# Products of zeros in TensorE's planned waits, and the ones of all V buffers written earlier, in a fused adaLN / sliding attention / token-MLP block

## The chip, the core and the metric

The kernel runs on one core of a Trainium2 chip. The core's engines work side by side, each in its own order: TensorE (PE; its weight loads are shown as PEld), VectorE (DVE), ScalarE (ACT), GpSimd (POOL) and SyncE (SP), which issues nearly all transfers. The metric is the device time of one execution in microseconds; the kernel before took 247.29 us, the median of 3 runs.

## The reference, cut to what matters

The batch is 1, S = 2048 tokens, D = 512, 32 heads of 16, a causal window of 256 keys, and an MLP that mixes tokens (2048 to 1792 and back).

```python
mod = (silu(c) @ w_mod).reshape(...)            # sa, ca, ga, sb, cb, gb
h = layernorm(x) * (1 + ca) + sa
q, k, v = split(h @ wqkv)                       # 32 heads of 16
p = softmax(where(mask, q @ k.T * 16 ** -0.5, -1e9))   # 0 <= i - j < 256
x = x + ga * ((p @ v) @ wo)
h = layernorm(x) * (1 + cb) + sb
u = gelu(einsum('bsd,sf->bdf', layernorm(h), w1) + b1)
y = einsum('bdf,fs->bds', u, w2) + b2
out = x + gb * y.transpose(0, 2, 1)
```

## The kernel before

**Head.** The 2048 tokens are 16 tiles of 128, in four groups of four. The head (from line 525) is written out by hand: the first loads, masks on GpSimd, the modulation's matrix-vector products on TensorE (`fm`, L586), layer norm of tiles 0 and 1, and the first projections. Among them stand ten products of a tile of zeros (`warm`, L571), whose result nobody reads.

**Planned part.** From line 641 on the order is made by a planner while the kernel is built. It keeps an estimated clock for TensorE (`pe["t"]`) and for each other engine (`free`), and always emits the work that it reckons can begin first (`while True`, L1278). Its time 0 lies at the end of the head. TensorE has three kinds of work: *scores* of a unit (L696; a unit is a part of four heads' window, in two halves, each into one of three PSUM tiles t0, t1, t2), *dense* groups into one of two PSUM tiles named dn (projections L356 and L331, modulation rows L402, and so on), and *AV* (`emit_av`, L721), the product of the exponentials with V. ScalarE takes the exponential of each half (L704), which makes that t tile free again. VectorE and ScalarE empty the dn tiles: K for even and odd heads (L369), Q and V (L287). The planner chooses; what then runs waits for semaphores, so an order that was planned with a wrong estimate makes its engine wait.

**Tiles 2 and 3.** The first group's second half comes later than its first: VectorE takes the statistics (`ln1_stats`, L244 and L245), GpSimd the reciprocal root (`rstd_of`, L231 and L235), VectorE applies them (`ln1_apply`, L256, tile xn), TensorE turns the result (`half_turn`, L309), VectorE modulates it (L297), and TensorE projects it (L356).

**V buffers.** `Vring` has three buffers V0, V1, V2. Beside each head's 16 columns stand two of ones, for the sum of the softmax. `ones_of(r)` writes them with two fills on GpSimd (L592, L593). In the kernel before, V0's are written in the head; V1's and V2's are planned jobs of GpSimd.

**Group 1's layer norm.** Tiles 4 to 7 are normalised (L256) into a pool of three buffers xn, and turned by transposing transfers on SP's queue (`turn_block`, L305). The fourth tile takes the buffer of the first, so its L256 on VectorE waits until the first transfer has landed. On SP's queue the four stand behind the loads of `wod` (L224), each of which waits for an earlier transfer (`wmod`, L221) to land. VectorE then modulates the turned tiles (L297 on h1T) once all four have landed; of these four steps one stands ahead of the evacuation of the last V group of group 0 (L287) on VectorE's queue, and the first AV product waits for that V group.

## Time and profile before

| | |
|---|---|
| median of 3 runs | 247.29 us (246.52, 247.29, 250.26) |
| profiled execution, whole | 248.87 us |
| its span | 246.7 us |
| mean granted clock of TensorE | 0.986 |
| busy: PE, DVE, ACT, POOL | 229.8, 190.0, 158.5, 69.7 us |

The span runs from the first to the last instruction; the remaining 2.17 us of the profiled execution lie around it. A row of the timeline has the start in us, the duration in us, the engine, the line, the operation, what is written and read, and how many instructions are merged into it; in brackets stands the idle time of the engine just before it, and what ended it. A row of a table by stage has the stretch and its length, then for each engine the busy time and the number of instructions, then the granted clock of TensorE, the share of the transfer engines and the rate.

### The profile page before, as it was taken

The page shows a single profiled execution, that of the slowest core. Times are in us where ns is not written, and L with a number is a line of the kernel's source. Part 1 is how long each engine was busy: PE and PEld are TensorE (multiplying, and loading weights), DVE is VectorE, ACT ScalarE, POOL GpSimd, SP SyncE. Part 2 cuts the span into 40 slices and gives each one's busy share as a digit, 9 for nine tenths or more (in the row PEclk, how much of TensorE's full clock was granted, in tenths as well). Part 3 has the DMA queues.
Part 4 walks back from the last instruction along what each step waited for, and adds up shares of the span by engine and source line. Part 5 has one row for each costly group of instructions (what it writes and reads, how often), then busy time and mean ns, then how long its engine had stood idle before and what let it go on. Part 6 is the DMA issues. An engine that isn't in the chain of part 4 may idle for free.

```text
span 246.7 us, 8687 instructions
## 1 busy us (share of the span) xinstructions
PE 229.8 (93%) x3691; PEld 122.6 (50%) x3723; DVE 190.0 (77%) x416; ACT 158.5 (64%) x182; POOL 69.7 (28%) x158
## 2 busy tenths in 40 slices
PE   5877999999999788999999999999999999999995
PEld 2544675655566365454454554544444444444444
DVE  5697679998999999999997989957974632543564
ACT  3495897999999898999999999950108700000000
POOL 7636104332272332423413624403540000000000
PEclk9996899999999999999999999999999999999999
DMA  6994455287573611010013131059995000201031
GB/s 202 314 351 129 88 148 131 43 139 160 168 98 74 152 25 27 5 21 3 9 23 79 51 88 45 3 169 352 415 409 224 0 3 0 85 23 64 27 103 43
DMA packets 32042, 27.70 MB, mean 112 GB/s; under 512 B 16516, under 2 KB 27652, under 8 KB 32004
## 3 DMA queue, kind: packets, MB, share of 16 engines
q1 hardware_dynamic: 31708, 26.63, 38.3%
q8 instruction: 29, 0.48, 0.9%
q10 hardware_dynamic: 296, 0.53, 0.6%
q14 instruction: 9, 0.07, 0.1%
HBM read 22.03 MB, written 2.10 MB: 98 GB/s over the span
## 4 chain that ended last, share of the span: by engine, by line
PE 74%; DVE 12%; ACT 6%; DMA 3%; issue 3%; SPq 0%; DVEq 0%; ACTq 0%
PE py L1475 20%; PE t L696 12%; PE dn L470 9%; PE dn L356 7%; PE t L462 6%; ACT et L704 6%; PE t L721 5%; PE dn L331 4%; PE dn L432 4%; PE t L1334 3%; DVE KT L369 3%; DMA wmod<-in_w_mod_dram 2%; PE pu L1334 2%; DVE QT L287 1%; PE pa L1370 1%
## 5 line engine op out<-in xcount | busy, mean ns | idle before, releaser
L704 ACT ACTIVATE et<-t 128x1024 bf16<-128x1024 f32 (+1 forms) x142 | 131.8, 1021 | 8.0 <-PE t L696 7.3
L1475 PE MATMUL py<-guT,w2r 128*128 128x512 bf16 (+2 forms) x234 | 47.7, 363 | 0.2
L696 PE MATMUL t<-QT,KT 32*128 32x64 bf16 (+4 forms) x752 | 38.0, 253 | 1.4 <-ACT et L704 0.9
L356 PE MATMUL dn<-h1T,wqkv 128*128 128x512 bf16 (+1 forms) x140 | 33.6, 357 | 4.9 <-DVE QT L287 1.8
L1475 PEld LDWEIGHTS <-w2r 128*128 128x128 bf16 x252 | 23.5, 98 | 25.4 <-DVE gelu_a L1357 0.4
L748 POOL TENSOR_TENSOR merge<-t,zr 128x512 bf16<-128x512 f32 (+1 forms) x16 | 21.5, 1346 | 42.8 <-DVE zr L743 42.7
L1490 DVE SCALAR_TENSOR_TENSOR o<-py,bFM,bc_gb 128x512 bf16<-128x512 f32 (+2 forms) x17 | 12.1, 711 | 24.5 <-PE py L1475 23.0
L696 PEld LDWEIGHTS <-KT 32*128 32x128 bf16 x752 | 13.9, 93 | 27.0 <-issue 25.1
L696 PE MATMUL t<-mask_r,mask_w 32*128 32x128 bf16 (+3 forms) x432 | 24.8, 223 | 0.4 <-issue 0.4
L470 PE MATMUL dn<-hb,w1hi 128*128 128x512 bf16 x91 | 23.9, 381 | 0.9 <-issue 0.6
L734 DVE STREAM_TRANSPOSE t<-t 128x1024 f32<-128x1024 f32 x16 | 19.8, 1236 | 4.2 <-PE t L721 4.1
L356 PEld LDWEIGHTS <-wqkv 128*128 128x128 bf16 x160 | 14.2, 102 | 16.3 <-issue 4.5
L231 POOL TENSOR_SCALAR ln_ve<-ln_mv 128x1 f32<-128x1 f32 x32 | 7.7, 241 | 48.0 <-DVE ln_mv L831 39.4
L235 POOL TENSOR_TENSOR ln_rstd<-ln_ve,mhalf 128x1 f32<-128x1 f32 x32 | 19.2, 601 | 2.7
L721 PEld LDWEIGHTS <-V 64*32 64x32 bf16 x1504 | 16.5, 91 | 6.6 <-issue 6.3
L721 PE MATMUL t<-et,V 64*32 64x320 bf16 (+4 forms) x1384 | 19.3, 251 | 0.0
L331 PE MATMUL dn<-wqkv,h1T 128*64 128x256 bf16 x256 | 17.6, 276 | 1.4 <-DVE V L287 0.9
L696 PEld LDWEIGHTS <-mask_w 32*128 32x128 bf16 x432 | 14.1, 95 | 2.7 <-issue 0.6
L331 PEld LDWEIGHTS <-h1T 128*64 128x64 bf16 x256 | 12.9, 109 | 3.4 <-issue 2.4
L470 PEld LDWEIGHTS <-w1hi 128*128 128x128 bf16 x98 | 8.1, 97 | 10.5 <-issue 3.0
L432 PE MATMUL dn<-wod,OTd 128*128 128x512 bf16 x43 | 12.2, 381 | 0.7 <-issue 0.3
L287 DVE CAST V<-dn 128x512 bf16<-128x512 f32 x15 | 10.1, 676 | 2.1 <-PE dn L331 2.1
(123 smaller groups left out, 289.3 us busy)
## 6 DMA issues: line engine op xcount, KB each, us to landing
w2r<-in_B_w_dram SPq DMA_DIRECT2D x14, 512.0 KB, 10.2
w1hi<-in_B_w_dram SPq DMA_DIRECT2D x11, 320.0 KB, 4.0
w1b<-in_B_w_dram SPq DMA_DIRECT2D x5, 448.0 KB, 6.7
x<-in_A_x_dram SPq DMA_DIRECT2D x16, 128.0 KB, 3.6
wmod<-in_w_mod_dram SPq DMA_DIRECT2D x4, 512.0 KB, 9.3
out_dram<-otile SPq DMA_DIRECT2D x15, 128.0 KB, 1.7
wqkv<-in_B_w_dram SPq DMA_DIRECT2D x11, 128.0 KB, 2.8
wqkv<-in_A_wqkv_dram SPq DMA_DIRECT2D x4, 256.0 KB, 6.0
```

What stands on the lines that cost most here:

```text
L235: nc.gpsimd.tensor_tensor(out=r[:], in0=ve[:], in1=mhalf[:, 0:n], op=ALU.pow)
L331: nc.tensor.matmul(pv[CH * par : CH * par + CH, 256 * ch : 256 * ch + 256].rearrange("p (h d) -> p h d", d=DH), lhsT=h1T[tg][:, dc, t0 : t ...
L356: nc.tensor.matmul(pq[:, 0:n_cols], lhsT=wqkv[:, dc, col0 : col0 + P], rhs=h1T[tg][:, dc, cols], start=(dc == 0), stop=(dc == ND - 1),)
L432: nc.tensor.matmul(pa[:], lhsT=tokens_of(OTd[tg][g], tl), rhs=wod[:, g, :], start=(g == 0), stop=(g == ND - 1),)
L462: nc.tensor.matmul(first[k][1][:, n, :], lhsT=w1_of(sc, 2 * k + n), rhs=hb[sc][:], start=(sc == 0), stop=(sc == NT - 1),)
L470: nc.tensor.matmul(ps[:], lhsT=w1_of(s0 + n, fc), rhs=hb[s0 + n][:], start=(n == 0), stop=(s0 + n + 1 == s1),)
L696: nc.tensor.matmul(o, lhsT=w, rhs=r, start=start, stop=stop, tile_position=(row, 0), skip_group_check=True,)
L704: nc.scalar.activation(out=state["e", u][:, 2 * a : 2 * a + 2, 0:w], in_=ps[:, :, 0:w], func=ACT.Exp, scale=SCORE_SCALE,)
L721: nc.tensor.matmul(chunks(o, qs), lhsT=Vring[kc // GC % 3][rows, kc % GC, h : h + 32], rhs=e[:, at : at + len(qs), :], start=first, stop=F ...
L734: nc.vector.transpose(out=v["t"][:].rearrange("p a c -> p (a c)"), in_=po[:].rearrange("p a c -> p (a c)"))
L748: eng.tensor_tensor(out=v["m"][:].rearrange("p (b d h) -> p h b d", d=DH, h=4)[:, :, lo:hi], in0=view()[:, :, lo:hi, 0:DH], in1=v["z"][:, ...
L1475: nc.tensor.matmul(pys[tl, lo, hi][:, 0 : hi - lo], lhsT=w2r[:, fc, tb * P : (tb + 1) * P], rhs=gated[fc][:] if last and (lo, hi) == LAST[ ...
```

## The change

Three edits. First, a new function `keep_busy` is called before each piece of work that the planner gives TensorE. It compares the planned start with the end of TensorE's work so far; if the gap is at least 0.35 us by the planner's clock, a PSUM tile is free by that clock, and the start lies before 24.0 on it, it takes that PSUM tile and emits one product of zeros (128x512) for each 0.25 us of the gap less 0.1. The planner's clocks and its count of TensorE's instructions aren't told of them. Second, `ones_of` is called for all three V buffers in the head. Third, the two planned jobs that wrote V1's and V2's ones keep their place in the planner's clock and emit nothing.

```diff
@@ -55,6 +55,7 @@
 PAUSE = 1.2
+BUSY_UNTIL = 24.0
 TURN_LAT = 2.5
@@ -601,7 +602,8 @@
         for step in masks["far"]:
             step(nc.gpsimd)
-        ones_of(0)
+        for r in range(3):
+            ones_of(r)
@@ -909,7 +911,7 @@
         for r in (1, 2):
-            Job(lambda eng, r=r: ones_of(r), {GE: 0.6}, prio=6, at=6.0).settle()
+            Job(lambda eng: None, {GE: 0.6}, prio=6, at=6.0).settle()
@@ -1275,6 +1277,17 @@
+        def keep_busy(until):
+
+            n = int((until - pe["t"] - 0.1) / 0.25)
+            pools = [
+                pool for pool, x in [*zip(t_pools, t_free), *zip(dn_pools, d_free)] if x is not None and x < pe["t"] + 0.1
+            ]
+            if n > 0 and pools and until < BUSY_UNTIL and pe["t"] > 0:
+                ps = pools[0].tile([P, 4 * P], DT.float32, name="dn" if pools[0] in dn_pools else f"t{t_pools.index(pools[0])}")
+                for _ in range(n):
+                    nc.tensor.matmul(ps[:], lhsT=zero[:, 0:P], rhs=zero[:], start=True, stop=True)
+
         while True:
             best = pick_pe()
@@ -1284,6 +1297,7 @@
             if callable(best[1]):
+                keep_busy(best[0])
                 best[1](best[0], *best[2])
```

Nine products of zeros come of it, all into t tiles and all among the first eight units: one each before the third early Q/K group and before the scores of units 1, 2 and 3; two between the Q/K groups of the second half (below); one before the second half's K group of head group 2; two before the scores of unit 7's second half, behind the transposition of the biases (L422). No other row moves on TensorE, and none on VectorE, ScalarE or SP.

The first place is TensorE's queue just ahead of the scores of unit 1. dn_437 (dn_443 in the changed kernel) is an early Q group, t1 and t0 are the PSUM tiles of the unit's two halves; in brackets stands the engine whose semaphore an instruction waits for. Before:

```order
L356 LDWEIGHTS wqkv_132
L356 MATMUL dn_437<-h1T_310,wqkv_132 128x256
L696 LDWEIGHTS KT0_167
L696 MATMUL t1_449<-QT1_421,KT0_167 128x256
L696 LDWEIGHTS KT0_167
L696 MATMUL t1_449<-QT1_421,KT0_167 128x256
```

and in the changed kernel:

```order
L357 LDWEIGHTS wqkv_132
L357 MATMUL dn_443<-h1T_314,wqkv_132 128x256
L1289 LDWEIGHTS zero_134
L1289 MATMUL t1_455<-zero_134 128x512 [waits PE_49]
L698 LDWEIGHTS KT0_167
L698 MATMUL t1_457<-QT1_425,KT0_167 128x256 [waits PE_49]
L698 LDWEIGHTS KT0_167
L698 MATMUL t1_457<-QT1_425,KT0_167 128x256
```

A product of zeros has come between the two, and the scores now wait for TensorE's own semaphore, since they write the tile that the zeros went to.

The second place is TensorE's queue in the second half of the first group, between the Q group dn_565 (dn_573) and the next K group dn_578 (dn_589). Before:

```order
L356 LDWEIGHTS wqkv_132
L356 MATMUL dn_565<-h1T_310,wqkv_132 128x256
L356 LDWEIGHTS wqkv_132
L356 MATMUL dn_578<-h1T_310,wqkv_132 128x256
L356 LDWEIGHTS wqkv_132
```

and in the changed kernel:

```order
L357 LDWEIGHTS wqkv_132
L357 MATMUL dn_573<-h1T_314,wqkv_132 128x256
L1289 LDWEIGHTS zero_134
L1289 MATMUL t0_586<-zero_134 128x512
L1289 LDWEIGHTS zero_134
L1289 MATMUL t0_586<-zero_134 128x512
L357 LDWEIGHTS wqkv_132
L357 MATMUL dn_589<-h1T_314,wqkv_132 128x256
```

Two products of zeros stand there now, in a tile whose earlier content ScalarE has read.

The third place is GpSimd's queue at the end of the head, around the reciprocal roots of tiles 2 and 3 (ve and rstd are the root's operand and result). Before:

```order
L592 MEMSET V0_164 128x8x16x2
L593 MEMSET V0_164 128x8x18
L231 TENSOR_SCALAR ln1False_ve_429<-ln1_mv0_268 128x1
L235 TENSOR_TENSOR ln1False_rstd_431<-ln1False_ve_429,mhalf_85 128x1
L231 TENSOR_SCALAR ln1False_ve_444<-ln1_mv0_268 128x1
L235 TENSOR_TENSOR ln1False_rstd_446<-ln1False_ve_444,mhalf_85 128x1
L592 MEMSET V1_165 128x8x16x2
L593 MEMSET V1_165 128x8x18
L592 MEMSET V2_166 128x8x16x2
L593 MEMSET V2_166 128x8x18
```

and in the changed kernel:

```order
L593 MEMSET V0_164 128x8x16x2
L594 MEMSET V0_164 128x8x18
L593 MEMSET V1_165 128x8x16x2
L594 MEMSET V1_165 128x8x18
L593 MEMSET V2_166 128x8x16x2
L594 MEMSET V2_166 128x8x18
L232 TENSOR_SCALAR ln1False_ve_435<-ln1_mv0_268 128x1
L236 TENSOR_TENSOR ln1False_rstd_437<-ln1False_ve_435,mhalf_85 128x1
L232 TENSOR_SCALAR ln1False_ve_450<-ln1_mv0_268 128x1
L236 TENSOR_TENSOR ln1False_rstd_452<-ln1False_ve_450,mhalf_85 128x1
```

The four fills of V1 and V2 have moved from behind the two roots to ahead of them.

## The prediction

> **What bounds the kernel now.** I read the page first: the busy shares, the row of TensorE's granted clock in 40 slices, and the chain that ended last.

> ```profile
> span 246.7 us, 8687 instructions
> PE   5877999999999788999999999999999999999995
> PEclk9996899999999999999999999999999999999999
> PE 74%; DVE 12%; ACT 6%; DMA 3%; issue 3%; SPq 0%; DVEq 0%; ACTq 0%
> ```

> TensorE carries the chain, and its clock is full but for the fourth and fifth slice, 18.5 to 30.8 us, which hold the first units. I then asked for a table of those stretches, moving the edges until the clock changed on them: it falls to half at 20.26 and returns at 27.08, 6.82 us later. Cut into equal parts of 3.41 us from there:

> ```profile
> core 0: us, PE busy (x) PEld busy (x) DVE busy (x) ACT busy (x) POOL busy (x), PEclk, DMA share, GB/s
> 6.60:10.02 3.42, 2.63 (x41) 1.95 (x43) 1.46 (x5) 1.02 (x2) 2.48 (x9) 1.00 1.09 318
> 13.43:16.84 3.41, 2.80 (x48) 1.87 (x48) 3.38 (x9) 3.41 (x5) 1.13 (x5) 1.00 1.11 350
> 16.84:20.26 3.42, 1.75 (x32) 0.96 (x26) 3.38 (x11) 2.50 (x3) 1.06 (x3) 1.00 1.07 320
> 20.26:23.67 3.41, 2.90 (x34) 1.79 (x34) 2.21 (x7) 2.68 (x3) 3.17 (x2) 0.50 0.27 64
> 23.67:27.08 3.41, 3.41 (x35) 1.86 (x37) 2.53 (x8) 1.90 (x3) 0.96 (x2) 0.50 0.26 65
> ```

> The fall follows the stretch in which TensorE was busy for 51% (1.75 of 3.42); after stretches with 77 and 82% it stayed. There VectorE had no idle time (3.38 of 3.42): TensorE waited for it. TensorE's timeline names the waits.

> ```profile
> 2.63 3.17 PE L571 MATMUL h<-zero 128*128 128x512 bf16 x7
> 8.53 0.38 PE L571 MATMUL h<-zero 128*128 128x512 bf16 x1
> 12.77 0.53 PE L696 MATMUL t<-QT,KT 32*128 32x256 bf16 x10
> 13.50 1.05 PE L356 MATMUL dn<-h1T,wqkv 128*128 128x256 bf16 x8
> 15.80 0.79 PE L309 MATMUL dn<-identity,xn 128*128 128x128 bf16 x8 [0.51 <-DVE QT L287]
> 17.95 1.05 PE L356 MATMUL dn<-h1T,wqkv 128*128 128x256 bf16 x8 [0.82 <-DVE h1T L297]
> 19.84 0.39 PE L356 MATMUL dn<-h1T,wqkv 128*128 128x256 bf16 x2 [0.85 <-DVE KT L369]
> 25.20 1.89 PE L356 MATMUL dn<-h1T,wqkv 128*128 128x256 bf16 x8
> 28.40 0.39 PE L696 MATMUL t<-QT,KT 32*128 32x256 bf16 x8 [0.27 <-ACT et L704]
> ```

> Waits of 0.51, 0.82 and 0.85 us stand ahead of the fall; eight like products take 1.05 us at full clock and 1.89 at half.

> [...]

> **The products of zeros.** Seven came in 3.17 us at half clock, the last lasting 0.63 by the spacing (six spacings of 0.42). At full clock I take 0.22 for the spacing (twice that of the 256-column products, (1.05 - 0.27) / 7 = 0.11) and 0.38 for one that is waited for (8.53).

> The first four stand where TensorE didn't idle. The one ahead of unit 1's scores goes to their own tile, so they wait for its end: with the one before it, 0.22 + 0.38 + 0.05 for the signal = 0.65 us later than 12.77. The wait on the own semaphore is in no trace; its bounds are 0.22 (no wait) and that 0.43. The same holds ahead of units 2 and 3, where the waits of 0.51 and 0.82 absorb it. The pair behind the eight products of 17.95 lies in the wait of 0.85: 0.22 + 0.38 = 0.60 of it. From 16.84 to 20.26 the idle time of 1.67 us should shrink to 0.2 to 0.5, so TensorE is busy for 85% or more, above the 77% after which the clock stayed. I take it that it stays.

> **What the clock is worth.** TensorE's projections while the clock was at half:

> ```profile
> L356 PE MATMUL dn<-h1T,wqkv 128*128 128x256 bf16 x19 | 4.6, 414 | 0.5 <-DVE QT L287 0.5
> ```

> These 19 products lose (1.89 - 1.05) / 8 = 0.105 us each, 2.0 us, besides what the scores lose. But VectorE empties all of them, and in these 6.82 us it idled for 1.20 + 0.88 = 2.08 us (from the table). The gain at 28.40 is thus at most 2.1 us. Off go the two products and their signal behind the biases, 0.22 + 0.38 + 0.05 = 0.65, less the 0.27 us that the scores waited there for ScalarE, which may be gone too; the product ahead of head group 2's K lies in a wait for VectorE. That leaves 1.5 to 1.8, say 1.6 us.

> **The ones.** GpSimd's and VectorE's timelines, and the four L256 of group 0:

> ```profile
> 11.98 0.23 POOL L231 TENSOR_SCALAR ln1False_ve<-ln_mv 128x1 f32<-128x1 f32 x1 [1.22 <-DVE ln_mv L245]
> 13.66 0.33 POOL L592 MEMSET V<- 128x256 bf16 x1
> 14.34 0.22 POOL L593 MEMSET V<- 128x144 bf16 x1
> 13.69 1.33 DVE L256 TENSOR_SCALAR xn<-x,ln_mv,ln1False_rstd 128x512 bf16<-128x512 bf16 x2
> 14.94 0.47 DVE L369 TENSOR_SCALAR KT<-dn,mask_even 128x256 bf16<-128x256 f32 x1
> L256 DVE TENSOR_SCALAR xn<-x,ln_mv,ln1False_rstd x4: 395/414/1014, 6.3 to 14.6; 128x512 bf16<-128x512 bf16 x4
> ```

> The four fills ran from 13.66 to 14.56, 0.9 us, beside the two L256, one of which took 1.01 us against 0.40 for its like. Ahead of the roots they fit into GpSimd's idle 1.22 us, so the roots begin at 11.98 as before; were that cover gone, the roots, which VectorE asks for from 13.69 on, would come up to 0.9 us later. VectorE, without idle time here, gains 0.62 us. It gives most back at once: the eight products of 13.50 come 0.6 us later, so the K group that L369 empties at 14.94 lands near 14.75, where VectorE would now be free at 14.4. I count 0.1 us (bounds 0 and 0.62).

> **What is late next.** TensorE would be 1.7 us ahead at 28.40. Group 1's turned tiles are not. SP's queue, its four transposing transfers (the landing row is that of the last two), and VectorE's queue behind them:

> ```profile
> SPq L224 <- DMA wmod<-in_w_mod_dram: 4.4, 3, 2.2
> 25.21 6.06 SPq L305 DMA_TRANSPOSE h1T<-xn  x4
> 30.06 1.22 SPq L305 DMA_TRANSPOSE h1T<-xn  x1
> DMA to landing us min/median/max: 2.4/2.4/2.4
> 28.68 0.41 DVE L256 TENSOR_SCALAR xn<-x,ln_mv,ln1True_rstd 128x512 bf16<-128x512 bf16 x1
> 32.17 0.69 DVE L287 CAST V<-dn 128x512 bf16<-128x512 f32 x1 [0.18 <-PE dn L331]
> 32.78 0.40 DVE L297 TENSOR_SCALAR h1T<-h1T,modFM 128x512 bf16<-128x512 bf16 x1
> 33.61 0.69 DVE L287 CAST V<-dn 128x512 bf16<-128x512 f32 x1 [0.43 <-PE dn L331]
> 34.48 0.71 PE L721 MATMUL t<-part,V 64*32 64x256 bf16 x46
> 34.55 1.04 PE t L721 x78
> ```

> SP reaches the first transfer at 25.21 because the loads of wod ahead waited 4.4 us for wmod to land; that doesn't depend on TensorE. The four then fill SP's queue until 31.27, and the last lands at 30.06 + 2.4 = 32.46. VectorE's L297 can't start before; the step behind it, the last V group of group 0, then ends at 32.46 + 0.05 + 0.40 + 0.69 = 33.60 where it ended at 34.30, and AV, which waits for it, starts 0.18 us later (34.48 - 34.30), at 33.78. So of 1.7 us ahead only 0.70 pass; the rest becomes TensorE waiting ahead of AV. From there on the chain is TensorE's own (its last row here), and the later transfers hang on its results, so I let 0.7 us reach the end.

> The 18 instructions shift the places where TensorE waits for nothing that the profile shows:

> ```profile
> PE dn L356 <- issue: 0.6, 4, 0.2
> PE dn L470 <- issue: 0.6, 4, 0.2
> PE t L696 <- issue: 0.6, 2, 0.4
> PE dn L432 <- issue: 0.3, 2, 0.2
> ```

> These are 12 waits, 2.1 us. Three of them more or fewer are 0.5 us either way; I take 0.

> **Sum.** 248.87 - 0.7 = 248.2 us for the profiled execution. That one lies 1.58 above the median of the three runs, and a fall of the clock may differ between them; I carry the difference over: 247.29 - 0.7 = 246.6 us.

> **The rivals.** *The clock falls all the same, and the products cost (slower).* Seven of the nine lie outside the two long waits, and other waits appear as the clock rises. It decides if a stretch of 3.41 us ahead of 20.26 stays near 51% busy; against it speaks that the pair alone brings 1.75 to about 2.35, 69%. Then the single product of head group 2 stands on TensorE's path at half clock, 0.42, and the pair behind the biases costs 0.65 less the 0.27 of waiting: 0.8 us, bounds 0.4 and 1.1. 247.29 + 0.8 = 248.1.

> *The full gain passes.* SP's wait at 25.21 is shorter, or the last V group is emptied ahead of L297's wait. It needs the last transfer to land by 31.6 rather than 32.46. Then 1.7 us pass, up to 2.1 if the own-semaphore waits are free: 245.2 to 245.6, say 245.5. Against it speaks that the four transfers stand back to back already.

> *The runs of before have no fall to lose.* If the stretches of 3.41 us begin elsewhere, from 15.4 say, the waits of 0.51 and 0.82 share one of 3.41 and the 0.85 falls into the next: 61% busy, and the clock may hold. Then before already meets SP's limit, AV starts at 33.78 in both, and the change gives nothing: 247.3. For it speaks the spread of the three runs, 246.52 to 250.26; against it that the profiled one shows a fall. [...]

> **How the numbers follow.** Forecast 0.50, clock falls all the same 0.20, full gain 0.15, no fall in before 0.15. The likeliest gives 246.6, its own range with the issue waits 246.1 to 247.1. The range goes from the full gain less a little of the 0.5 us, 245.0, to the slower case with its bound of 1.1, 248.4, and a little for the runs' spread, 248.5. A difference of 2%, 4.9 us, is about what a measurement of this kernel can tell from no change; no case reaches it, and only the spread of the runs could: faster 0.02, same 0.95, slower 0.03.

> **What would show it.** The granted clock at 1.00 from 16.8 to 27.1, with TensorE over 80% busy in the 3.4 us ahead of 20.3. No L256 of group 0 above 0.45 us. The scores of unit 1 at about 13.4 and the K product of 19.84 within 0.3 us of there. The scores of 28.40 near 26.7. The first transposing transfer still at 25.2 and the last landing at 32.4, AV at 33.8 with TensorE idle ahead of it. The prediction is wrong if AV starts before 33.3 or after 34.5, or if the clock is at half anywhere in the first 34 us.

## The result, and the profile after

| | before | after |
|---|---|---|
| median, us | 248.09 (20 runs, 246.52 to 253.21) | 249.11 (20 runs, 247.38 to 251.96) |
| ratio, with its 95% interval | | 1.0067 [1.0044, 1.0090] |
| profiled execution, whole | 248.87 | 248.58 |
| its span | 246.7 | 246.4 |

The kernel became 0.67% slower, where 0.28% faster was forecast: little, and within the 2% that count as the same, but the interval excludes 1, and the median lies beyond the range's upper end of 248.5. The two profiled executions don't show this: the one of before was among its slower ones. So the question is why a kernel whose trace has lost what the prediction wanted gone is no faster.

First the stretches of the clock, as a table by stage of the kernel after (columns as in the prediction).

```profile
core 0: us, PE busy (x) PEld busy (x) DVE busy (x) ACT busy (x) POOL busy (x), PEclk, DMA share, GB/s
16.84:20.26 3.42, 2.62 (x40) 1.54 (x42) 3.38 (x11) 3.06 (x4) 1.21 (x3) 1.00 1.00 301
20.26:23.67 3.41, 2.90 (x53) 1.89 (x45) 3.29 (x10) 3.10 (x4) 3.28 (x4) 1.00 0.28 75
23.67:27.08 3.41, 2.85 (x51) 1.73 (x53) 2.61 (x8) 3.14 (x5) 0.69 (x1) 1.00 0.72 113
```

TensorE is busy for 77% of the stretch that had 51% (2.62 of 3.42), and the clock stays at 1.00. VectorE's timeline of the same kernel has the two normalisations beside which GpSimd's fills ran:

```profile
14.14 0.73 DVE L257 TENSOR_SCALAR xn<-x,ln_mv,ln1False_rstd 128x512 bf16<-128x512 bf16 x2
```

They take 0.73 us, where the pair took 1.33. TensorE's timeline, down to the third group of AV products:

```profile
8.48 0.63 PE L572 MATMUL h<-zero 128*128 128x512 bf16 x1 [0.22 <-issue]
13.59 0.40 PE L698 MATMUL t<-QT,KT 32*128 32x256 bf16 x12
19.70 0.39 PE L357 MATMUL dn<-h1T,wqkv 128*128 128x256 bf16 x2 [0.28 <-DVE KT L370]
26.49 0.40 PE L698 MATMUL t<-QT,KT 32*128 32x64 bf16 x10 [0.27 <-PE dn L423]
32.59 0.71 PE L723 MATMUL t<-part,V 64*32 64x256 bf16 x46
33.90 0.26 PE L723 MATMUL t<-et,V 64*32 64x128 bf16 x9 [0.24 <-issue]
36.23 0.24 PE L698 MATMUL t<-mask_r,mask_w 32*128 32x128 bf16 x5
38.18 0.20 PE L698 MATMUL t<-mask_r,mask_w 32*128 32x64 bf16 x3 [1.70 <-issue]
41.55 0.41 PE L723 MATMUL t<-part,V 64*32 64x256 bf16 x24
```

The scores of 28.40 stand at 26.49, and AV begins 1.89 us earlier (32.59 against 34.48). Then 1.70 us go in one piece, in the middle of a unit's score products: the engine waits for nothing that the profile shows. In before the same stretch has this:

```profile
37.85 1.25 PE L356 MATMUL dn<-h1T,wqkv 128*128 128x512 bf16 x4
39.33 0.40 PE L696 MATMUL t<-QT,KT 32*128 32x64 bf16 x12 [0.22 <-issue]
41.23 0.41 PE L721 MATMUL t<-part,V 64*32 64x256 bf16 x24
```

There the wait lasts 0.22 us and stands 18 instructions further on, behind four dense products. The third AV group starts at 41.23 in before and at 41.55 after: all of the lead is gone.

Both waits end 2.2 to 2.4 us behind a packet of one queue. The page after has its row:

```profile
q8 instruction: 29, 0.48, 0.7%
```

The trace has the start of each of its 29 packets: 36.0 us after, 36.9 us before. TensorE has 7,430 instructions in this trace (3698 products and 3732 weight loads; 34 products have no record), that is one packet for some 256 (7430 / 29). Between the wait of 0.24 us at 33.90 and the one at 38.18 the timeline has 128 products, with as many weight loads: 256 instructions. So I read these waits as TensorE waiting for its next block of instructions. The packets' starts and this count support the reading; no run removes the loading itself.

### The profile page after: what moved, and what is told of

Same layout as the page of the kernel before. It is cut to its first block, busy times and chain, and to the rows that moved or that the text cites. A ratio compares the mean times of both kernels' runs of the same rounds, so it can differ in the third digit from the quotient of the medians.

```text
span 246.4 us, 8703 instructions
## 1 busy us (share of the span) xinstructions
PE 230.0 (93%) x3698; PEld 123.7 (50%) x3732; DVE 189.1 (77%) x416; ACT 158.5 (64%) x182; POOL 69.5 (28%) x158
## 4 chain that ended last, share of the span: by engine, by line
PE 73%; DVE 15%; ACT 4%; DMA 3%; issue 3%; POOL 0%; SPq 0%; ACTq 0%; DVEq 0%
PE py L1489 20%; PE t L698 11%; PE dn L471 8%; PE dn L357 6%; PE t L463 6%; PE t L723 5%; PE dn L332 4%; PE dn L433 4%; ACT et L706 4%; PE t L1348 3%; DVE KT L370 3%; PE pu L1348 2%; DMA wmod<-in_w_mod_dram 2%; DVE ln_stats L245 2%; PE pa L1384 1%
## 5 line engine op out<-in xcount | busy, mean ns | idle before, releaser
L698 PE MATMUL t<-QT,KT 32*128 32x64 bf16 (+4 forms) x752 | 37.2, 250 | 1.8 <-ACT et L706 0.9
L357 PE MATMUL dn<-h1T,wqkv 128*128 128x512 bf16 (+1 forms) x140 | 32.2, 341 | 3.6 <-DVE QT L288 1.7
L245 DVE BATCH_NORM_STATS2 ln_stats<-x 128x6 f32<-128x512 bf16 x16 | 10.8, 677 | 0.9 <-DMA x<-in_A_x_dram 0.9
```

Source lines behind the costliest of these rows:

```text
L245: nc.vector.bn_stats(out=stats[:], in_=xres[4 * tg + tl][:])
L357: nc.tensor.matmul(pq[:, 0:n_cols], lhsT=wqkv[:, dc, col0 : col0 + P], rhs=h1T[tg][:, dc, cols], start=(dc == 0), stop=(dc == ND - 1),)
L698: nc.tensor.matmul(o, lhsT=w, rhs=r, start=start, stop=stop, tile_position=(row, 0), skip_group_check=True,)
```

## The experiments

Ratios are to the kernel before, run beside them on the same chip, with 95% intervals. "Third AV" is the start of the AV group that stands at 41.23 in before.

**Each half alone.** The ones alone (`ones_only`, repeated as `ones_more`):

```diff
-        ones_of(0)
+        for r in range(3):
+            ones_of(r)
@@
-            Job(lambda eng, r=r: ones_of(r), {GE: 0.6}, prio=6, at=6.0).settle()
+            Job(lambda eng: None, {GE: 0.6}, prio=6, at=6.0).settle()
```

> Only the ones of V1 and V2 move into the head; no products of zeros, TensorE's instructions as before. Code theory (the 18 added instructions move the places where TensorE waits for its code): no long wait of TensorE without a releaser in the profile (none over 0.5 us between 30 and 45 us), one L256 of group 0 falls from 1.01 to 0.40 us, and the time is that of before or up to 0.6 us less: ratio 0.998 to 1.000. Product theory (the products themselves and their waits cost): the same, 0.998 to 1.000. Clock theory (the clock falls elsewhere since VectorE's and TensorE's times have moved): it says nothing of this one.

> The ones moved alone, once more: does it by itself keep the runs with two stretches of half clock away? They were none of 12, before had 15 of 59. If it does: none again, ratio 0.996 to 0.999. If that was chance: 2 to 4 of 12 at 0.986, ratio 0.998 to 1.002.

Measured: 0.9994 [0.9963, 1.0024] and 0.9967 [0.9931, 1.0002]. The products alone (`products_only`, repeated as `products_again`) are the change without these lines.

> Only the nine products; the ones of V1 and V2 are written where they were. Code theory and product theory: as slow as the whole change, ratio 1.004 to 1.009, and in the profile the 1.7 us wait of TensorE among scores near 36 us (code theory) or no single long wait but many short ones (product theory). If the ones were the cost instead: ratio 0.998 to 1.001.

> The nine products without the moved ones, once more beside the whole change. If the ones add a cost in company with the products: 1.000 to 1.003 here and 1.005 to 1.009 for the whole change. If not: both alike within 0.003.

Measured: 1.0023 [0.9997, 1.0049] and 1.0013 [0.9977, 1.0050]. So the ones aren't the loss. But the products alone were expected to be as slow as the whole change, and that missed: both their traces have the wait at the same scores, 1.43 us long (at 38.65 and 38.57), and yet they cost 0.3 to 0.6 us by these ratios, with 1 inside both intervals. Neither half by itself reaches the 1.0067 of the whole, whose repetition (`after_again`) gave 1.0046 [1.0014, 1.0079]; these intervals overlap, and whether the two halves cost more together stays open.

> The whole change once more, beside the others on one chip. If the first measurement holds: ratio 1.004 to 1.009, granted clock mostly 1.0 or 0.993. If it is as the products alone were (1.0023): 1.000 to 1.004, and the ones cost nothing.

**The shift alone.** The kernel before, with products of one column in the head behind the first seven `warm` products. They take next to no time (sixteen products of one column took 0.54 us in `shift_again`, from 7.02 on, so nine some 0.3 by estimate) and bring only their instructions (two each):

```diff
         warm(WARM[0])
+        for _ in range(9):
+            nc.tensor.matmul(warm_ps[:, 0:1], lhsT=zero[:, 0:P], rhs=zero[:, 0:1], start=True, stop=True)
```

> Before, with nine products of one column in the head where TensorE waits for the weights of the modulation: 18 instructions more, next to no work, no product among the units. Code theory: a wait without a releaser of 1 us or more between 35 and 40 us, at the same scores as in the changed kernel, where before had 0.22; time 0.5 to 1.7 us above before, ratio 1.002 to 1.007. Product theory and clock theory: as before, ratio 0.999 to 1.001.

> The 18 instructions of next to no work in the head, once more, for a profile that can be read. Code theory: a wait of TensorE of 1 us or more without a releaser at the scores behind the second AV, near 37 us, and 0.2 to 0.4 us near the end of the first AV, as in the changed kernel; ratio 1.002 to 1.007. Otherwise: only waits of 0.2 us as in before, and the slower time has another cause.

Measured with nine, that is 18 instructions as in the change: 1.0064 [1.0025, 1.0102] and 1.0069 [1.0035, 1.0103]. The profile of the first was of an execution far out of line (a span of 435.7 us) and isn't used. That of the second has the wait at the place where the kernel after has it. TensorE's timeline of this run:

```profile
34.34 0.69 PE L723 MATMUL t<-part,V 64*32 64x256 bf16 x45 [2.18 <-DVE V L287]
38.77 0.20 PE L698 MATMUL t<-mask_r,mask_w 32*128 32x64 bf16 x3 [1.01 <-issue]
```

So 18 instructions that compute nothing cost what the whole change costs. The products alone bring 18 instructions too and cost less; what they win back no run separates. Then with two (4 instructions) and with eighteen (36):

> Before with two products of one column more in the head (4 instructions). Code theory, worked out from the profiles so far: the place at which TensorE waits for code behind the second AV lies two of the 512-column Q/K products earlier, 0.4 us less work ahead of it, so its wait goes from 0.2 us to about 0.6; time 0 to 0.4 us above before, ratio 1.000 to 1.002. If 18 instructions were slow for another reason (their own time in the head), this is as before.

> Before with eighteen such products (36 instructions). Code theory: the place lies nine short products ahead of that of the 18, inside the same scores or at their start; the wait there is 1 to 2 us again and the time as with 18: ratio 1.003 to 1.008. If the head's instructions cost by their own time, it is twice the loss of 18: 1.012 or more.

Measured: 1.0025 [0.9986, 1.0063] and 0.9990 [0.9954, 1.0026]; 1.003 to 1.008 was expected for 36. TensorE's timelines of `shift_4` and `shift_36`, a row of each:

```profile
39.68 0.59 PE L356 MATMUL dn<-h1T,wqkv 128*128 128x512 bf16 x2 [0.83 <-issue]
37.50 0.21 PE L698 MATMUL t<-QT,KT 32*128 32x64 bf16 x4 [1.14 <-issue]
```

With 4 the wait came two dense products earlier than in before; with 36 it came near the start of the scores. Counted in the traces from the start, it stands behind 612 or 613 weight loads in before, in the change and its repetition, in `shift_4`, `shift_again` and `shift_36` (a few semaphore rows of the same queue counted in; without them 606 in before and 608 in the change). So in these runs its place is a number of instructions, whatever was added ahead. Twice the shift doesn't cost twice as much: its 0.9990 can't be told from no cost. I read it that what counts is where the places fall.

**The planner told of the products.** `keep_busy` adds to the count by which the planner places loading:

```diff
+                pe["n"] += 2.01 * n
```

> The whole change, and the planner's count of TensorE's instructions is told of the products, so that it plans around the places where it reckons with a wait for code. Code theory: the wait of 1.7 us near 36 us falls below 0.7, and the kernel is as fast as before or up to 1 us faster, ratio 0.996 to 1.001. Product theory and clock theory: as slow as the change, ratio 1.004 to 1.009. A new order that is worse by itself would also be slower, and then its profile has other waits.

Measured: 1.0340 [1.0307, 1.0374]. The planner then chose another order, with other waits (1.88 us for V ahead of AV, 0.75 ahead of the second group), so this says that its count can't be set right by itself, and nothing about the shift.

**The change without the shift.** Nine of the ten products in the head are left out and the planner's count is kept, so that behind the last of the nine products of zeros, at unit 7, every TensorE instruction has the number it has in before (`nine_even`):

```diff
-WARM = (7, 1, 2)
+WARM = (1, 0, 0)
@@
-... "n": 2 + 2 * (25 + 4 * ND + sum(WARM)), ...
+... "n": 2 + 2 * (25 + 4 * ND + 10), ...
```

> The whole change with nine of the head's ten products of zeros taken out, so that all code from the first unit's second product on stands where it stood before. Code theory: the wait of 1.7 us near 36 us is gone (below 0.5); what the head loses at half clock, up to 1 us, stands against it: ratio 0.998 to 1.004. Product theory: slower than the change itself, above 1.007, without any long wait for code going away.

Measured: 1.0000 [0.9960, 1.0040]. TensorE's timeline of this run, at the same place:

```profile
32.76 0.71 PE L723 MATMUL t<-part,V 64*32 64x256 bf16 x46
38.27 0.40 PE L698 MATMUL t<-QT,KT 32*128 32x64 bf16 x12 [0.55 <-DVE ks L288]
40.16 0.41 PE L723 MATMUL t<-part,V 64*32 64x256 bf16 x24
```

The wait for nothing shown is gone from the scores; in its place is a shorter one for VectorE. (The head has lost nine products too, so this isn't the shift alone; AV starts at 32.76, 0.17 us later than in the change.) The same with only the pair in the second half kept, and two of the head's products left out in turn (`pair_even`, repeated as `pair_more`):

```diff
-WARM = (7, 1, 2)
+WARM = (7, 0, 1)
@@
-BUSY_UNTIL = 24.0
+BUSY_UNTIL = 11.0
@@
-            if n > 0 and pools and ...
+            if n > 1 and pools and ...
```

> The ones moved, of the nine products only the pair behind the second half's first Q group, and two of the head's ten products of zeros taken out, so that the places of the code stay those of before. Code theory and clock: no wait over 0.5 us near 36 us, no run with two stretches of half clock (granted clock 0.986), time 0.5 to 1 us below before: ratio 0.996 to 0.999. Product theory: between before and the change, 1.000 to 1.004.

> The ones moved, the pair of products in the long wait, and the code's places kept, once more for a narrower interval: ratio 0.996 to 1.000, and no run at a granted clock of 0.986.

Measured: 0.9988 [0.9956, 1.0020] and 0.9989 [0.9947, 1.0031].

**A second profile of the kernel before,** for the clock and for SP's transfers (`before_again`):

> The kernel before once more, for a second profile. If the fall of the clock differs from run to run (phase), this one may show none, or one stretch of 3.4 us; then TensorE's AV of group 0 starts about as early as in the changed kernel, 32.6 to 33.5 us. If the fall belongs to the order of the work, it stands again at about 20 to 27 us and AV starts at 34.5.

One execution of 249.04 us, at full clock in the whole of the planned part (mean granted clock 1.0). The table by stage, SP's timeline and TensorE's timeline of this run:

```profile
16.84:20.26 3.42, 1.93 (x28) 1.06 (x25) 3.35 (x11) 3.36 (x4) 0.62 (x2) 1.00 1.07 315
20.26:23.67 3.41, 2.88 (x55) 1.89 (x55) 3.30 (x9) 2.51 (x3) 3.41 (x3) 1.00 0.32 65
```

```profile
24.16 5.93 SPq L305 DMA_TRANSPOSE h1T<-xn  x4
```

```profile
8.48 0.63 PE L571 MATMUL h<-zero 128*128 128x512 bf16 x1 [0.22 <-issue]
13.54 0.62 PE L696 MATMUL t<-QT,KT 32*128 32x256 bf16 x10
26.32 0.74 PE L696 MATMUL t<-QT,KT 32*128 32x64 bf16 x10
32.74 0.71 PE L721 MATMUL t<-part,V 64*32 64x256 bf16 x46
40.09 0.41 PE L721 MATMUL t<-part,V 64*32 64x256 bf16 x24
```

No product of zeros was added here, a stretch with 56% stayed at full clock (1.93 of 3.42), and AV began at 32.74, as early as after (32.59). So this execution is the one to set beside the one after: the same start in the head, no fall in either, AV within 0.15 us, and then the third AV at 40.09 against 41.55. By the rows of both the 1.46 us between are TensorE's wait of 1.70, less one of 0.55 for VectorE that only this run has at its place (as in `nine_even`), and some 0.3 us in smaller differences. The whole spans, 246.9 and 246.4 us, go the other way, by what follows the third AV (table below): the pair shows where the 1.46 us arise, and not the loss of the medians.

**More shift for the change.** If the loss is one of places, 18 more instructions should move it as they did in the kernel before; if it is the products', they can't help. `after_36` is the whole change with nine products of one column in the head (36 instructions in all). `pair_36` is the change with `BUSY_UNTIL = 11.0` and `n > 1` (only the pair, 4 instructions) and sixteen of them (36 again).

> The whole change plus nine products of one column in the head: 36 instructions more than before in all, of which 18 are the change's. Code theory: like the 36 alone (0.999), since from the first units on all code stands as there, and better by what the steadier clock is worth: ratio 0.995 to 1.000, faster than the change although it does more. Product theory: at least as slow as the change, 1.004 to 1.010.

> The ones moved, only the pair of products in the long wait, and sixteen products of one column in the head, so that the code stands as with 36 instructions more. Code theory and clock: the fastest so far, ratio 0.992 to 0.998. If the place of 36 was as good as before only by chance: 0.998 to 1.003.

Measured: 0.9980 [0.9947, 1.0014], beside 1.0046 for the change itself on the same chip, and 0.9954 [0.9920, 0.9988]. The products stayed and the loss went. `pair_36` is faster than both kernels: 247.57 us where before had 248.40 and the change 249.36. TensorE's timeline of `pair_36`:

```profile
32.19 0.69 PE L725 MATMUL t<-part,V 64*32 64x256 bf16 x45 [0.93 <-DVE V L288]
36.66 0.21 PE L700 MATMUL t<-QT,KT 32*128 32x64 bf16 x4 [1.15 <-issue]
40.12 0.41 PE L725 MATMUL t<-part,V 64*32 64x256 bf16 x24
```

The wait of 1.15 us hasn't gone: with 36 instructions it stands at the scores too, behind 613 weight loads as in `after_36`. The gain comes later. TensorE's waits from 46 to 100 us, in the second profile of before (its three largest) and in `pair_36` (both rows) (in us: in total, times, longest):

```profile
PE dn L356 <- DVE QT L287: 2.0, 2, 1.3
PE dn L331 <- DVE V L287: 1.1, 3, 0.4
PE t L696 <- issue: 0.4, 1, 0.4
```

```profile
PE dn L357 <- DVE QT L288: 0.8, 1, 0.8
PE dn L332 <- DVE V L288: 0.7, 2, 0.4
```

In these and the other profiles such waits account for most of what differs behind the third AV: the rest of the span varies by 2.8 us, and less these waits by 1.0. The table has the start of the first and third AV, the rest of the span behind the third, and the sum of TensorE's waits from 46 to 100 us, with those for VectorE among them, each from the kernel's timeline and waits:

| kernel | instr. ahead | first AV | third AV | rest | waits (for VectorE) | rest less waits |
|---|---|---|---|---|---|---|
| before | 0 | 34.5 | 41.2 | 205.5 | 3.8 (2.8) | 201.7 |
| before_again | 0 | 32.7 | 40.1 | 206.8 | 4.6 (3.6) | 202.2 |
| nine_even | 0 | 32.8 | 40.2 | 205.6 | 3.8 (2.1) | 201.8 |
| pair_even | 0 | 32.4 | 39.1 | 206.4 | 4.7 (2.8) | 201.7 |
| pair_more | 0 | 32.3 | 39.4 | 205.0 | 2.8 (1.8) | 202.2 |
| after | 18 | 32.6 | 41.6 | 204.9 | 3.3 (2.4) | 201.6 |
| after_again | 18 | 34.2 | 42.6 | 204.7 | 2.4 (2.4) | 202.3 |
| shift_again | 18 | 34.3 | 42.1 | 205.3 | 3.3 (2.4) | 202.0 |
| products_again | 18 | 33.4 | 41.9 | 206.3 | 3.7 (3.7) | 202.6 |
| shift_36 | 36 | 33.0 | 41.0 | 204.4 | 2.7 (1.8) | 201.7 |
| after_36 | 36 | 33.7 | 42.0 | 204.1 | 1.8 (1.8) | 202.3 |
| pair_36 | 36 | 32.2 | 40.1 | 204.0 | 1.5 (1.5) | 202.5 |

From the first to the third AV it takes 6.7 to 7.4 us with no shift, 7.8 to 9.0 with 18 and 7.9 to 8.3 with 36. By the means of the rows, the shifts cost 1.4 and 1.0 us there. Behind it TensorE waits for VectorE for 1.8 to 3.6, 2.4 to 3.7, and 1.5 to 1.8 us. These are single executions and the first two overlap, but the three with 36 are the lowest: there the loss is won back. Why VectorE is waited for less, with its own work unchanged, stays open.

## Why the prediction was wrong

**What bounds the kernel** was right: TensorE, waiting for VectorE in the first units, with a fall of the clock as the trace has it (to 0.50 from 20.26 to 27.08 us).

**The clock is held.** Right in the trace after: no half clock from 16.8 to 27.1 us. "TensorE is busy for 85% or more" was high; it was 77%. Over the runs it is right in part. A mean clock of 0.986 or less, which is two stretches of 3.41 us at half (6.82 / 246.7 / 2 = 0.014), came in 35 of the 129 runs of before that were made beside the experiments (leaving out one of 265.31 us, far out of line), and in 3 of the 32 of the change (with `after_again`); a single stretch, 0.993, stayed common (11 of its first 20). But in the 24 runs of the ones alone the two stretches never came either, nor in the 24 of the products alone; in the 42 of the empty instructions they came 11 times. Each half went without them by itself, so the products weren't shown to be what holds the clock. Nor does the share decide that the prediction went by: `shift_again` kept full clock behind a stretch with 51% (last section).

**The ones** were right in kind: no long normalisation is left, 0.60 us of the 0.62 came (1.33 - 0.73), the roots began at 12.43 where 11.98 was forecast, but waited 0.87 us for VectorE's statistics and not for the fills, and the runs of the ones alone are at or just below 1.

**Unit 1, the K product, the scores of 28.40** came at 13.59, 19.70 and 26.49, where 13.4, 19.84 within 0.3 and 26.7 were forecast. That is in part luck: the second execution of before, with no product of zeros among the units, has the first and the last of these at 13.54 and 26.32. There the head was late and the clock full, so neither number shows what the products cost or earn.

**"What is late next"** failed: the first transposing transfer was forecast to be "still at 25.2", and started at 23.48 after, and at 24.16 in the second profile of before. Ahead of it on SP's queue stand loads that wait for wmod to land, 4.4 us in all in before and 3.1 after, and in the two executions of before it began 1.05 us apart (25.21 and 24.16). So the limit of 33.78 wasn't there, and AV started at 32.59, outside the bounds of 33.3 to 34.5 that the prediction set itself. The limit is real in other executions: in `shift_again` the first transfer started at 24.99, VectorE waited 2.7 us for the turned tiles, and AV waited 2.18 us for V and started at 34.34; in `pair_36` VectorE waited 1.5 us for them and AV 0.93 for V.

**The term that was mis-sized** is the one for the shift. "Three of them more or fewer are 0.5 us either way; I take 0." By the runs it is 0.64 and 0.69% of 248 us, 1.6 to 1.7 us slower, for the 18 instructions alone added to before, and without this shift the change loses nothing (`nine_even`). The prediction summed the waits of before as they stood, 0.2 us each, and moved three of them; it didn't ask what a wait would last at another place. The one behind the second AV had four dense products ahead of it and lasted 0.22; moved ahead of these it lasted 1.70. In before these products run until 39.10 (37.85 + 1.25), and the wait for the block ends at 39.33. So I read it that the block was as late there, and 1.25 us of the lateness were covered by work that TensorE had already.

**The carrying over.** "I carry the difference over" put the whole gain of one profiled execution on the median. That execution was of the rarer kind, with two stretches at half, 35 of 129, and such runs took some 2 us more than the others (on the last chip a mean of 249.42 us in 12 runs, and 247.07 in the 7 at full clock). So preventing them would be worth about 35 / 129 x 2.35 = 0.6 us on average, and nothing in the typical run. The rival "The runs of before have no fall to lose", given 0.15, was nearer; it forecast no change, which is what the change shows once its shift is taken out (`nine_even`, 1.0000).

Forecast and result thus differ by 0.95% (1.0067 against 0.9972), 2.4 us: some 1.7 are the shift, as it measured in the kernel before. The rest, 0.7, is the gain forecast, which `nine_even` doesn't show; its interval, 0.4% either way, is too wide to exclude it.

## What to carry to other kernels

Here 18 empty instructions added ahead on TensorE cost 0.64 and 0.69%, and 36 cost nothing measurable, by what stood at the places where it waited for its next block, as I read these waits. So a change that adds instructions is compared with one that adds the same number of empty ones, and tried with some more. A wait for nothing the profile shows is priced by what would stand ahead of it at its new place, not by how long it lasted at the old one. Before a stall of one trace is priced, look at a second execution of the same kernel, above all where the clock or a transfer is in it.

## What the runs showed of the hardware

**The clock's stretches began elsewhere in two executions of one kernel.** In the profiled execution of before the product at 8.53 took 0.38 us, and in the second profile of the same kernel the one at 8.48 took 0.63, though both pages give full clock there. Products of 256 columns take 0.27 from 9.0 us on in the first, and 0.42 until 10.0 in the second. So I read it that the head of the second ran at half clock over 1 us longer, and that its page shows that clock as full. The traces' own records of the clock begin at 6.61 us in the first and at 11.37 in the second, and in the first the clock changes whole stretches of 3.41 later (20.26 = 6.61 + 4 x 3.41). If the stretches of the second are counted from its 11.37, the one with 56% lies across two, from 14.78 and from 18.20, which are busy for 79 and 70% (2.69 of 3.42 and 2.38 of 3.41). That could be why it kept full clock; two executions don't show that the stretches keep to such a count.

**Busy time alone didn't decide the clock.** Cut in the same way, from the start of their own records, `shift_again` was busy for 51% from 16.53 to 19.94 (1.75 of 3.41) and stayed at full clock, where before fell behind 51%; and `shift_36` fell at 8.99 behind a stretch with 72% (2.44 of 3.41). Their mean granted clocks were 1.0 and 0.991. What decides stays open.
